# Storing x2's rows: two DMAs of 64 partitions in place of one with an outermost dimension of 2

## The chip, the cores and the metric

The kernel runs on one core of a Trainium2 chip. The metric is the device time of one execution in microseconds, the median of three runs. Before the change it is 1280.42 us (1277.43 to 1281.81).

## The reference

Three stages, one behind the other. Attention over 4 batches of 8 heads, 1152 positions and 64 features, with queries that are means of two neighbours (so 576 of them); a product stage (a * b) @ w3 @ w_out; and eight experts, to which 2304 tokens are assigned greedily by their logits, 288 each.

```python
# attention
q_pool = q.reshape(B, H, S // 2, 2, D).mean(axis=3)
attn = softmax(q_pool @ k.T / sqrt(D))            # written out in the reference
x = (attn @ v).transpose(0, 2, 1, 3).reshape(2304, 512)
# products
x = ((x @ w1) * (x @ w2)) @ w3 @ w_out            # 512 -> 1024 -> 1024 -> 512
# experts: every expert gets cap = 2304 / 8 tokens, in the order of the logits
logits = x @ w_gate
for idx in argsort(-logits.flatten()):
    tok, e = idx // 8, idx % 8
    if assigned[tok] < 0 and counts[e] < cap: assigned[tok] = e; counts[e] += 1
for e in range(8):
    out[assigned == e] = relu(x[assigned == e] @ w1[e]) @ w2[e]
```

## The kernel before

All products are made from operands split into a high and a low part (three matmuls for one product). Every operation is recorded with the buffers that it reads and writes, and a list scheduler (class `Sched`) orders all of them with rough costs and latencies that are written at each `sch.op`; they are then emitted in order of their modelled start. So each engine has a fixed order, and a changed cost or latency moves the order of operations on all engines. Nearly all instructions of this part are recorded through one helper, so the profile puts them on line 113, and they are told apart by the names of their tiles.

The part that the change touches stands between the product stage and the experts. `x2 = h @ W`, with W = w3 @ w_out, is made in 18 tiles of 128 tokens (`x2_part`). A tile's products add up in a bank (`pb`), ACT copies it to a buffer `x2o` of three (`r_xo`), and SP stores it to DRAM twice: the left 256 columns to `x2a`, all 512 columns to `x2` (the profile calls it `x`). The rows of a tile are two groups of 64, whose tokens lie 9 rows apart in DRAM, so a store had the pattern [2, 64, width] on the DRAM side and 128 partitions on the other. The last three tiles (15, 16, 17) are made half by half: first the left columns of each, then the right columns of 16, 17 and 15 (`late`), whose operands for tile 15 are split once more by ACT (`x2h`) and DVE (`x2l`).

The experts fetch their tokens' rows from DRAM with gathers that POOL issues. The first expert's rows come in halves: three gathers from `x2a` into `early`, which need every row of `x2a`, and three from `x2` (by `idx_right`) into `g`, which need every row of `x2`. PE transposes them, ACT and DVE split them (`exh`, `exl`), and the products of seven groups of features with the left half are placed ahead of the transposes of the right half (`AHEAD`). Gathers of the weights (`u`) stand behind them on POOL.

All along, the greedy assignment (`routing`, tiles `rt_...`) runs beside it: seven phases, each with eight rounds in which DVE makes a mask, PE counts (`rt_oh`, `rt_mask`), DVE reduces, PE sums (`rt_own`), and DVE takes the next threshold; then `rt_rows`, and a list of an expert's tokens (`sl_...`) which gives `idx`. Four phases end by the end of x2, the other three beside the experts. Each engine takes its instructions in order, so a routing product waits on PE behind what stands ahead of it, and the other way round.

The lines of the profile for the parts below are those of the kernel printed here.

Of the kernel before, what the change touches and what calls it, by code (L numbers as in the profile page):

```python
# [11 lines left out]
F32 = mybir.dt.float32  # L12
# [5 lines left out]
OP = mybir.AluOpType  # L18
AX = mybir.AxisListType
PSUM = bass.MemoryType.PSUM  # L20

B, H, S, D = 4, 8, 1152, 64
SP = S // 2
# [11 lines left out]
class Region:  # L35
    """a tile pool that opens and closes while the ops are emitted; its tiles are made at their first use"""
# [36 lines left out]
class LazyTag(Lazy):  # L73
    """a tile of a tag, whose buffers are used in turn"""
# [11 lines left out]
class TagRing:  # L86
    """the buffers of a tag, in turn; the ops that touch the tiles first keep the tiles' order"""
# [4 lines left out]
    def next(self, shape, dt, name, key):  # L92
        """a tile whose ops know it by key and (key, 1), and those keys of the tile that had its buffer before"""
        self.keys.append(key)
        n = len(self.keys) - 1
        free = [self.keys[n - self.bufs], (self.keys[n - self.bufs], 1)] if n >= self.bufs else []
        return LazyTag(self.region, shape, dt, name, self.tag, self.bufs), free
# [20 lines left out]
class LazyCore:  # L118
    """the engines of the core, taking Lazy tiles as operands"""
# [21 lines left out]
class Slots:  # L141
    """n buffers given out while the emission is ordered"""
# [5 lines left out]
class Hold:  # L148
    """one use of a buffer of Slots: taken by its first op, given back after its last"""
# [13 lines left out]
class Sched:  # L163
    """Orders the emission: ops are created in program order with the buffers they read and write;
    run() list-schedules them on the engines with rough costs and emits them by start time."""
# [9 lines left out]
    def ctl(self, fn, labels=(), after=()):  # L175
        """runs fn while emitting, once every op with one of the labels has been emitted"""
        gate, self.gate = self.gate, []
        o = self.op("CTL", 0.0, fn, after=after, lat=0.0)
        self.gate = gate
        o.label = "ctl"  # L180
        o.sdeps = {x for x in self.ops if x.label in labels}
        return o
# [162 lines left out]
def attention(nc, tc, sch, pool, prep, s_pt, s_s, ident, xT, rsum, q, k, v):  # L345
    """xT[4*b + hp][:, s*64 + p] = attention rows of heads (2hp, 2hp+1), query p*9+s of batch b."""
# [54 lines left out]
    def both(ps, hi, lo, src, n, r, kh, kl, pr, scale=None):  # L401
        """hi and lo of scale * src in PSUM; each of several places (place, key) gets them from there"""
# [12 lines left out]
    def prepare_q(p, pr):  # L415
        """qst[p][:, x, h]: q's high part over its low part (x = 0), or the other way round, for s = 0..3, 5..8;
        diag[p]: the high and the low part of both heads' s = 4, each head in its quarter"""
# [9 lines left out]
        # pairs of rows are added, transposed (s above s+5), scaled by -1/16 = -(1/2)(1/8), and split  # L427
# [25 lines left out]
        if first:  # L453
            for g in range(2):
# [14 lines left out]
                # the other head's by way of SBUF; the bank's readers take turns only once  # L469
# [27 lines left out]
        # columns: s = 0..3 (above 5..8) of the one head, then of the other  # L497
# [11 lines left out]
    def prepare_k(p, pr):  # L509
        """kst[p, h]: rows of k's high part over its low part; khl[p]: the high and the low part, head 1 below head 0"""  # L510
# [3 lines left out]
        if p == 0:  # L514
            # the first head's by itself, which is there sooner
# [54 lines left out]
    def tile_ops(p, j, sm, pr):  # L570
# [14 lines left out]
        for c in range(3):  # L585
# [5 lines left out]
            sch.label = "prep" if j == 4 else "attn"  # the ops that read the tiles of the preparation  # L591
# [7 lines left out]
            # the copy that finds the row's least value on its way  # L599
# [8 lines left out]
        for g in range(3):  # L608
# [25 lines left out]
            if (j, g) in RAW:  # L634
                # by way of a copy in SBUF, which frees the vector engine
# [136 lines left out]
NCG = 6           # columns of tokens whose counts one matmul takes  # L772
# [3 lines left out]
def routing_consts(nc, pool, spare):  # L776
    """constants of the routing, made on the chip, by way of a buffer that is not in use yet"""
# [13 lines left out]
    nc.vector.tensor_scalar(tri, jp, 0.0, None, op0=OP.is_le)          # [p', p]: p' >= p  # L791
    c["tris"] = tris = pool.tile([128, 128], BF16, name="rc_tris")
    nc.vector.tensor_scalar(tris, jp, 0.0, None, op0=OP.is_gt)         # [p', p]: p' < p
# [18 lines left out]
    # of the counts [(a, t), (a', e)] those with a = a'; and each row's own threshold  # L812
# [14 lines left out]
    # thresholds of the first round: the keys as float bits  # L827
# [4 lines left out]
    # rows (in token order) of column c*128+p: 576*b + 9*(p%64) + s with (b, s) = divmod(2*c + p//64, 9)  # L832
# [20 lines left out]
def routing(nc, sch, rp, slots, c, L, keyL, A, rows_of, idx, prio, prio_l):  # L853
    """Greedy assignment, in which every expert gets N/8 tokens: A[p, e, c] = 1 where token c*128+p goes to expert e.

    Every phase fills an expert. The n-th in the order of filling has its weights in rows rows_of[n][p, k] of 1024
    values, and idx[n][r, g] = row of its token 96*g + r."""
# [32 lines left out]
    def pick(n):  # L890
        """the n-th expert: the first one that is full and not taken yet"""
# [10 lines left out]
    for ph in range(8):  # L902
# [18 lines left out]
        if ph < 7:  # L921
            # the counts lack what the experts can take
            dve(120, lambda: nc.vector.tensor_scalar(
                own8[96:97], rem[96:97, None, :].to_broadcast([1, NTHR, 8]), 4096.0, -1.0, op0=OP.min, op1=OP.mult), [keyR], ["own8r"])
            base = kb = None  # float bits of the lower end of the range that holds the threshold
# [143 lines left out]
def slot_lists(nc, sch, rp, slots, c, A, idx, prio, prio_l):  # L1069
    """lists(n, own): idx[n][r, g] = row of token 96*g + r of the expert that own (one-hot) names"""  # L1070
# [59 lines left out]
KF = 8           # tiles of 128 of the 1024 hidden features  # L1130
KD = DM // 128
CH = 288         # tokens in a chunk of the first products
NCH = N // CH
LC = 384         # tokens in a chunk of the logits
# [4 lines left out]
def moe_and_experts(tc, sch, env, w1, w2, w3, w_out, w_gate, e1, e2, out):  # L1139
# [13 lines left out]
    def split(hi, lo, src, n, pr, r, wh, wl, hi_e=("ACT", "DVE"), lo_e=("DVE", "POOL"), uses=(), hold=None, free=()):  # L1153
        """hi = src rounded to the matrix unit's 12 bits, lo = src - hi (exact)"""
# [9 lines left out]
    def acc_op(engine, dur, fn, r, hold, first, pr, then=()):  # L1164
        """one of the ops that add up in a bank, for which the buffers in `then` are free already"""
        if first:
            return sch.op(engine, dur, fn, r=r, w=then, takes=hold, prio=pr)
        o = sch.op(engine, dur, fn, r=r, w=[hold], prio=pr)
        o.uses.append(hold)
        hold.users += 1  # L1170
        return o

    # ---- weights that come as float64: their float32 values, made from the words of the float64
# [10 lines left out]
    def convert(w, row, col, blocks, width, pr):  # L1184
        """[128, blocks*width] float32: w[row + 128*j + p, col:col + width] for j in range(blocks)"""
# [11 lines left out]
        # sign, exponent less 896 and 23 bits of the mantissa; what float32 can't hold becomes 0  # L1197
# [27 lines left out]
    def split_x(b, pr):  # L1225
        """x = xhi + xlo; xhi goes to the buffer of a part of x that has been split"""
# [11 lines left out]
    # ---- h = (x @ w1) * (x @ w2), kept whole, and its routing logits  # L1238
# [45 lines left out]
    def logits(f, c, pr):  # L1284
        """rows 16*c.. of one bank: the stationary is w_gate's columns between columns of zeros"""
# [13 lines left out]
    # w_gate seen from the hidden features: Wg = w3 @ (w_out @ w_gate)  # L1299
# [10 lines left out]
    def project(nm, weight, copy, rows_n, cols, stat, stat_key, put_hi, put_lo, dst_key, step):  # L1310
        """hi | lo of weight @ (stat hi + lo); the parts of w_out, and those of w3 transposed, go to DRAM as well"""
# [71 lines left out]
    lg_part = lambda c, n: lg.rearrange("p c t -> p (c t)")[:LW, c:c + n].bitcast(F32)  # noqa: E731  # L1383
    sch.op("ACT", c_act(LC), lambda: evac("ACT", lg_part(0, LC), lg_ps.tile[:LW, :LC]), uses=[lg_ps], w=[klg], prio=P_H)

    # ---- routing beside W = w3 @ w_out and x2 = h @ W
# [4 lines left out]
    # the logits leave the region of the products before it closes  # L1391
# [27 lines left out]
    # W  # L1419
# [38 lines left out]
    # x2, its rows in token order in DRAM  # L1458
# [4 lines left out]
    whole = [(x, m) for m in range(KF) for x in ("Wh", "Wl")]  # what all but two tiles wait for, as W needs banks too  # L1463
    r_xh, r_xl = ring(xr, "x2h", 2, [128, KF, 128], F32R), ring(xr, "x2l", 2, [128, KF, 128], F32R)
    r_xo = ring(xr, "x2o", 3, [128, DM], F32)
    LAST = N // 128 - LATE  # the last tiles are made half by half, so that the first expert's rows are there sooner

    def x2_part(t, h, n, xs, xo, pr):
        """columns h * n.. of the rows of tile t"""
# [12 lines left out]
        for dst, w, width, key in ((x2a, DM // 2, DM // 2, "x2a"), (x2, DM, n, "x2")):  # L1482
            def fn(dst=dst, w=w, width=width, at=b * SP + s_, step=(b1 - b) * SP + s1 - s_):
                nc.sync.dma_start(dram(dst, at * w + h * n, [[step * w, 2], [NS * w, 64], [1, width]]), xo[:, h * n:h * n + width])
            if key == "x2" or not h:
                sch.op("DMA", 600, fn, r=[(kxo, h)], w=[(key, t, h)], prio=pr, lat=2500)
# [21 lines left out]
    # ---- the experts  # L1508
# [13 lines left out]
    def unit(w, n, k, pr):  # L1522
        """rows rows_of[n][:, k] of w, split: the tiles of the two halves of the parts, and their keys"""
# [47 lines left out]
    def gather(e, pr):  # L1571
        xh, kxh = r_xh()
        xl, kxl = r_xl()
        # the rows' halves: [h][j] = place, key
# [33 lines left out]
    def expert(e, xs, wu, pr):  # L1608
# [42 lines left out]
        # the last expert's rows go out as soon as the last of their quarters is there  # L1651
# [23 lines left out]
    # the first expert's rows come half by half  # L1675
# [8 lines left out]
    for e in range(8):  # L1684
        if e + 1 < 8:
            xs[e + 1] = gather(e + 1, P_E + e + 0.4)
            wu_next = lambda e=e: expert_w(e + 1, P_E + e)  # noqa: E731
# [14 lines left out]
NX = B * KD       # x in parts of [128 features, one batch]  # L1702
# [7 lines left out]
AHEAD = 7          # groups of features that the first halves of the first expert's rows keep busy  # L1710
HELD = 4           # loads of weights that the gathers of the first expert's rows don't have to wait for
LATE = 3           # tiles of x2 made half by half
# [57 lines left out]
```

## Time and profile before

| what | value |
|---|---|
| time, median of three runs | 1280.42 us (1277.43 to 1281.81) |
| profiled execution, span from first to last instruction | 1286.7 us (no time around it is given) |
| PE busy | 1176.8 us, 91% |
| DVE busy | 1033.4 us, 80% |
| SP's stores of x2 | 837.6 to 975.8 us of the span |
| stretch in which the experts start | from 978.9 us |
| mean granted clock of PE | 0.965 |

The profiled execution is 6.3 us longer than the median of the runs, so positions in the trace are read as positions in it, and a difference is carried over to the median. A row of a timeline gives start and length, and in brackets how long the engine was idle ahead of it and what ended that. SP rows are the issue of a DMA; a long one means that SP was held while issuing. The granted clock is 1.00 at 2.4 GHz and 0.50 at 1.2 GHz.

### The profile page before, as it was taken

How to read it: one execution, taken by the hardware profiler on the slowest of the kernel's cores; microseconds unless marked ns; L12 is line 12 of the kernel's file. 1: busy time of each engine (PE TensorE's matmuls, PEld its weight loads, DVE VectorE, ACT ScalarE, POOL GpSimd, SP SyncE). 2: the span in 40 equal slices, each digit the busy share in tenths (PEclk: the TensorE clock that was granted, in tenths of full speed). 3: DMA queues.
4: the chain of work that ended last, by engine and by line, in shares of the span. 5: the costliest groups of instructions: out<-in, count | busy, mean ns of one | idle time of the engine just before them, and what ended most of it. 6: DMA issues, size and time to landing. Idle time of an engine off the chain costs nothing.

```text
span 1286.7 us, 23991 instructions
## 1 busy us (share of the span) xinstructions
PE 1176.8 (91%) x8377; PEld 1106.5 (86%) x8377; DVE 1033.4 (80%) x2964; ACT 636.6 (49%) x1333; POOL 683.8 (53%) x704
## 2 busy tenths in 40 slices
PE   7999999999999999899999999888984978989895
PEld 5999999999999998899999996666673978879895
DVE  7999999999999989988777866777762797978651
ACT  6888888888888886422222102222220443432330
POOL 4566666666666655444322533454423786763860
PEclk9999999999999999899999999999996999988998
DMA  9676766666766531254655234411113545552440
GB/s 211 150 180 149 156 159 155 155 145 148 155 145 156 117 73 57 83 189 164 196 174 182 72 122 138 127 59 51 51 51 104 162 150 170 179 169 68 138 150 19
DMA packets 115445, 169.85 MB, mean 132 GB/s; under 512 B 46789, under 2 KB 78540, under 8 KB 115324
## 3 DMA queue, kind: packets, MB, share of 16 engines
q1 hardware_dynamic: 102940, 125.32, 37.2%
q0 software_dynamic: 12384, 43.00, 10.6%
q8 instruction: 66, 1.08, 0.4%
q14 instruction: 55, 0.45, 0.1%
HBM read 104.87 MB, written 24.45 MB: 101 GB/s over the span
## 4 chain that ended last, share of the span: by engine, by line
PE 68%; DVE 19%; DMA 4%; issue 3%; SPq 2%; POOL 2%; ACT 1%; POOLq 0%; DVEq 0%; ACTq 0%
PE pb L113 29%; PE s L590 11%; PE pt L614 7%; PE pt L113 6%; PE pt L664 6%; PE s L664 5%; PE s L614 3%; DMA u<-in_moe_w_dram,rows 2%; DVE ul L113 2%; SPq L113 2%; DVE cv_v L113 1%; DVE p L600 1%; DVE rt_own L113 1%; DVE sl_oh L113 1%; DVE rt_flag L113 1%
## 5 line engine op out<-in xcount | busy, mean ns | idle before, releaser
L600 DVE TENSOR_SCALAR_CACHE_REDUCE p<-s 128x384 f32<-128x384 f32 x432 | 229.7, 550 | 34.5 <-PE pt L614 12.0
L590 PE MATMUL s<-kst,qst 128*128 128x384 f32 x768 | 199.3, 358 | 4.8 <-DVE p L600 3.2
L605 ACT ACTIVATE p<-p,mn 128x1152 f32<-128x1152 f32 x144 | 181.2, 1258 | 25.0 <-DVE mn L603 22.8
L113 PE MATMUL pb<-xhi,wh 128*128 128x288 f32 x512 | 156.6, 306 | 1.7 <-ACT wh L113 1.7
L113 PE MATMUL pb<-xlo,wh 128*128 128x288 f32 x512 | 152.3, 297 | 3.3 <-DVE xlo L113 3.3
L113 PE MATMUL pb<-xhi,wl 128*128 128x288 f32 x512 | 152.0, 297 | 1.4 <-DVE wl L113 1.4
L590 PEld LDWEIGHTS s<-kst,qst 128*128 128x128 f32 x768 | 122.9, 190 | 11.1 <-DVE p L600 9.7
L614 PE MATMUL pt<-ident,p 128*128 128x128 f32 x879 | 132.1, 272 | 0.3 <-ACT p L605 0.3
L648 DVE TENSOR_TENSOR p_lo<-pt,p_hi 128x384 fp32r<-128x384 f32 x230 | 124.5, 550 | 0.7 <-ACT p_hi L331 0.7
L331 ACT ACTIVATE p_hi<-pt 128x384 fp32r<-128x384 f32 x230 | 106.7, 493 | 11.3 <-PE pt L614 11.1
L614 PEld LDWEIGHTS pt<-ident,p 128*128 128x128 f32 x879 | 106.8, 140 | 4.4 <-ACT p L605 0.5
L113 DVE SCALAR_TENSOR_TENSOR cv_v<-cv_raw,cv_v 128x512 int32<-128x512 int32 (+1 forms) x120 | 102.1, 856 | 6.9 <-POOL cv_raw L113 4.9
L113 PEld LDWEIGHTS pb<-xlo,wh 128*128 128x128 f32 x512 | 97.3, 190 | 4.1 <-DVE xlo L113 4.1
L113 PEld LDWEIGHTS pb<-xhi,wh 128*128 128x128 f32 x512 | 97.2, 190 | 2.5 <-ACT wh L113 1.9
L113 PEld LDWEIGHTS pb<-xhi,wl 128*128 128x128 f32 x512 | 97.2, 190 | 1.8 <-DVE wl L113 1.8
L341 POOL TENSOR_TENSOR p_lo<-praw,p_hi 128x384 fp32r<-128x384 f32 x96 | 96.9, 1018 | 0.4
L113 ACT ACTIVATE a<-pb 128x288 f32<-128x288 f32 x64 | 26.2, 410 | 133.0 <-PE pb L113 126.8
L335 POOL CAST p_hi<-praw 128x384 fp32r<-128x384 f32 x96 | 47.6, 506 | 81.9 <-ACT praw L331 81.9
L113 POOL TENSOR_TENSOR cv_raw<-cv_raw 128x512 f32<-128x512 f32 x40 | 43.2, 1079 | 86.3 <-DVE cv_v L113 67.1
L113 POOL DMA_INDIRECT u<-in_moe_w_dram,rows x64 | 73.6, 1150 | 27.1 <-issue 8.6
L113 PE MATMUL pb<-ehh,uh 128*128 128x288 f32 x256 | 80.7, 315 | 0.0
L113 ACT ACTIVATE uh<-u 128x1024 fp32r<-128x1024 f32 (+1 forms) x66 | 55.4, 861 | 51.1 <-DMA u<-in_moe_w_dram,rows 50.8
(317 smaller groups left out, 3479.5 us busy)
## 6 DMA issues: line engine op xcount, KB each, us to landing
cv_raw<-in_moe_w_dram SPq DMA_DIRECT2D x32, 512.0 KB
vr<-in_v_dram SPq DMA_DIRECT2D x32, 288.0 KB
kr<-in_k_dram SPq DMA_DIRECT2D x32, 288.0 KB
kst<-kH SPq DMA_DIRECT2D x31, 288.0 KB
kst<-kL SPq DMA_DIRECT2D x31, 288.0 KB
qr<-in_q_dram SPq DMA_DIRECT2D x15, 576.0 KB
w3t<-wg SPq DMA_DIRECT2D x16, 512.0 KB
w<-w3t SPq DMA_DIRECT2D x16, 512.0 KB
```

Source lines behind the costliest of these rows:

```text
L113: return f(*[x.get() if isinstance(x, Lazy) else x for x in a], **{n: x.get() if isinstance(x, Lazy) else x for n, x in k.items()})
L331: nc.scalar.activation(out, in_, AF.Copy)
L335: nc.gpsimd.tensor_copy(out, in_)
L341: (nc.vector if eng == "DVE" else nc.gpsimd).tensor_tensor(out, a, b, op=OP.subtract)
L590: nc.tensor.matmul(ps.tile[:, :384], a[:, :], b[:, cs], start=(n == 0), stop=(n == len(passes) - 1))
L600: sch.op("DVE", c_dve(384), lambda ps=ps, c=c, cs=cs: nc.vector.tensor_scalar(t[:, cs], ps.tile[:, :384], 1.0, BIG, op0=OP.mult, op1=OP.mi ...
L605: sch.op("ACT", c_act(S, psum=False, acc=True), lambda: nc.scalar.activation(t, t, AF.Exp, bias=mn[:, 3:4], scale=-1.0, accum_out=sm[0][:, ...
L614: nc.tensor.transpose(ps.tile[:, a * 128:(a + 1) * 128], t[:, b * 128:(b + 1) * 128], ident)
L648: sch.op("DVE", c_dve(384), lambda view=view, src=src: nc.vector.tensor_tensor(view(lo), src(), view(hi).bitcast(F32), op=OP.subtract), us ...
L664: nc.tensor.matmul(ps.tile[:, :n], vt[:, t, :, :], src[half][:, t, off:off + n], start=(half == 0 and t == 0), stop=(half == 1 and t == NT ...
```

## The change

In `x2_part` the store with a pattern of [2, 64, width] becomes two stores of 64 partitions each, with the rows as outermost dimension. The cost in the scheduler becomes 500 with a latency of 2300, where it was 600 and 2500. Both stores are recorded as writing the same key, so the scheduler takes the second of a pair to depend on the first, and emits it later. Else the diff removes comments and docstrings, which emit nothing.

```diff
         for dst, w, width, key in ((x2a, DM // 2, DM // 2, "x2a"), (x2, DM, n, "x2")):
-            def fn(dst=dst, w=w, width=width, at=b * SP + s_, step=(b1 - b) * SP + s1 - s_):
-                nc.sync.dma_start(dram(dst, at * w + h * n, [[step * w, 2], [NS * w, 64], [1, width]]), xo[:, h * n:h * n + width])
-            if key == "x2" or not h:
-                sch.op("DMA", 600, fn, r=[(kxo, h)], w=[(key, t, h)], prio=pr, lat=2500)
+            if key == "x2a" and h:
+                continue
+
+            for rows, at in ((slice(0, 64), b * SP + s_), (slice(64, 128), b1 * SP + s1)):
+                def fn(dst=dst, w=w, width=width, rows=rows, at=at):
+                    nc.sync.dma_start(dram(dst, at * w + h * n, [[NS * w, 64], [1, width]]), xo[rows, h * n:h * n + width])
+                sch.op("DMA", 500, fn, r=[(kxo, h)], w=[(key, t, h)], prio=pr, lat=2300)
```

The end of SP's stores, tiles 15 to 17 (their buffers are x2o0, x2o1 and x2o2), before:

```order
L113 DMA x2a_217<-x2o0_9760 2x64x256 [waits DMAHW1_49,Activation_49]
L113 DMA x2_216<-x2o0_9760 2x64x256 [waits DMAHW2_49]
L113 DMA x2a_217<-x2o1_9818 2x64x256 [waits DMAHW3_49,Activation_49]
L113 DMA x2_216<-x2o1_9818 2x64x256 [waits DMAHW4_49]
L113 DMA x2a_217<-x2o2_9877 2x64x256 [waits DMAHW5_49,Activation_49]
L113 DMA x2_216<-x2o2_9877 2x64x256 [waits DMAHW6_49]
L113 DMA x2_216<-x2o1_9818 2x64x256 [waits DMAHW7_49,Activation_49]
L113 DMA x2_216<-x2o2_9877 2x64x256 [waits DMAHW0_49,Activation_49]
L113 DMA x2_216<-x2o0_9760 2x64x256 [waits DMAHW1_49,Activation_49]
```

and now, from the first store of tile 17's left columns on:

```order
L113 DMA x2a_217<-x2o2_9881 64x256 [waits DMAHW5_49,Activation_49]
L113 DMA x2a_217<-x2o1_9820 64x256 [waits DMAHW6_49]
L113 DMA x2_216<-x2o1_9820 64x256 [waits DMAHW7_49]
L113 DMA x2_216<-x2o2_9881 64x256 [waits DMAHW0_49]
L113 DMA x2_216<-x2o1_9820 64x256 [waits DMAHW1_49,Activation_49]
L113 DMA x2a_217<-x2o2_9881 64x256 [waits DMAHW2_49]
L113 DMA x2_216<-x2o2_9881 64x256 [waits DMAHW3_49]
L113 DMA x2_216<-x2o2_9881 64x256 [waits DMAHW4_49,Activation_49]
L113 DMA x2_216<-x2o1_9820 64x256 [waits DMAHW5_49]
L113 DMA x2_216<-x2o2_9881 64x256 [waits DMAHW6_49]
L113 DMA x2_216<-x2o0_9760 64x256 [waits DMAHW7_49,Activation_49]
L113 DMA x2_216<-x2o0_9760 64x256 [waits DMAHW0_49]
```

A wait named Activation is for the copy of a new half tile; DMAHW is for the store eight places ahead. Before, the last left-half store waits for its own copy alone. Now its second part (x2a from x2o2, sixth row) stands behind a store of tile 16's right columns, which waits for that copy.

PE where x2 ends and the first expert begins, before:

```order
L113 MATMUL pb_6478<-Wh,x2l_9184 128x256
L113 MATMUL pb_6478<-Wh,x2h_9171 128x256
L113 MATMUL pb_6478<-Wl,x2h_9171 128x256
L113 MATMUL pb_6478<-Wh,x2l_9184 128x256
L113 MATMUL pt_65<-ident,early 128x96 x3
L113 MATMUL pt_67<-ident,early 128x96 x3
L113 LDWEIGHTS rt_mask_9280
L113 MATMUL pt_66<-rt_oh_9232,rt_mask_9280 90x48
```

and now:

```order
L113 MATMUL pb_6478<-Wh,x2l_9184 128x256
L113 LDWEIGHTS rt_mask_9280
L113 MATMUL pt_65<-rt_oh_9232,rt_mask_9280 90x48
L113 LDWEIGHTS rt_mask_9280
L113 MATMUL pt_65<-rt_oh_9232,rt_mask_9280 90x48
L113 LDWEIGHTS rt_mask_9280
L113 MATMUL pt_65<-rt_oh_9232,rt_mask_9280 90x48
L113 MATMUL pt_67<-ident,early 128x96 x3
L113 MATMUL pt_66<-ident,early 128x96 x3
L113 LDWEIGHTS rc_ones_145
L113 MATMUL pt_68<-rt_own_9188,rc_ones_145 128x120
```

A round of routing (`rt_mask`, then `rt_own`) that stood behind the transposes of the first gathered rows stands around them. Up to the transposes PE's order is otherwise the same; behind them, routing stands earlier among the products of the experts: the last three `rt_rows` come after 201, 549 and 864 of the 1,536 products, where it was 258, 618 and 969. ACT, DVE and POOL follow with their parts.

## Rows read from the trace of the kernel before

**Rows 1.** page of the profile, first part and chain of waits

```profile
PE 1176.8 (91%) x8377; PEld 1106.5 (86%) x8377; DVE 1033.4 (80%) x2964; ACT 636.6 (49%) x1333; POOL 683.8 (53%) x704
PE 68%; DVE 19%; DMA 4%; issue 3%; SPq 2%; POOL 2%; ACT 1%; POOLq 0%; DVEq 0%; ACTq 0%
```

**Rows 2.** stretches: length, busy us (count) per engine, granted clock, DMA share, GB/s

```profile
660.00:680.00 20.00, 20.00 (x171) 19.66 (x170) 14.65 (x27) 4.72 (x10) 4.30 (x5) 1.00 0.61 195
860.00:880.00 20.00, 16.48 (x93) 12.69 (x92) 18.23 (x64) 4.61 (x8) 8.87 (x9) 0.99 0.14 51
960.00:970.00 10.00, 5.13 (x29) 4.63 (x29) 6.19 (x30) 2.10 (x6) 0.00 (x0) 0.74 0.14 50
970.00:980.00 10.00, 0.42 (x1) 0.18 (x1) 0.00 (x0) 0.00 (x0) 3.74 (x6) 0.50 0.23 74
```

**Rows 3.** timeline of the SP queue: start us, length us, store issued

```profile
837.59 0.58 SPq L113 DMA_DIRECT2D x2a<-x2o  x1
838.22 0.50 SPq L113 DMA_DIRECT2D x<-x2o  x1
962.60 2.58 SPq L113 DMA_DIRECT2D x2a<-x2o  x1
965.22 10.57 SPq L113 DMA_DIRECT2D x<-x2o  x4
```

**Rows 4.** tile x2o: issue lengths of its stores, ns min/median/max

```profile
L113 SPq DMA_DIRECT2D x<-x2o x21: 494/2572/4871, 838.2 to 973.3; - x21
L113 SPq DMA_DIRECT2D x2a<-x2o x18: 478/486/3291, 837.6 to 962.6; - x18
```

**Rows 5.** timeline of ACT, in brackets idle time ahead and its releaser

```profile
959.75 0.38 ACT L113 ACTIVATE x2o<-pb 128x256 f32<-128x256 f32 x1 [7.52 <-DMA x<-x2o]
966.30 0.38 ACT L113 ACTIVATE x2o<-pb 128x256 f32<-128x256 f32 x1 [4.59 <-PE pb L113]
```

**Rows 6.** timeline of PE, end of x2 and start of the experts

```profile
956.98 0.28 PE L113 MATMUL pb<-Wl,x2h 128*128 128x256 f32 x1
957.10 0.28 PE L113 MATMUL pb<-Wh,x2l 128*128 128x256 f32 x1
960.70 0.38 PE L113 MATMUL pb<-Wh,x2h 128*128 128x256 f32 x1 [3.32 <-ACT x2h L113]
978.85 0.42 PE L113 MATMUL pt<-ident,early 96*128 96x96 f32 x1 [12.58 <-DMA early<-x2a,idx]
981.39 0.90 PE L113 MATMUL pt<-ident,early 96*128 96x96 f32 x4 [0.77 <-DMA early<-x2a,idx]
995.85 0.74 PE L113 MATMUL pt<-ident,g 96*128 96x96 f32 x3 [2.02 <-issue]
```

**Rows 7.** timeline of POOL, the gathers of the first expert

```profile
974.04 0.95 POOL L113 DMA_INDIRECT early<-x2a,idx  x1 [19.21 <-DMA x2a<-x2o]
985.58 0.93 POOL L113 DMA_INDIRECT g<-x,idx_right  x1 [7.09 <-issue]
```

**Rows 8.** timeline of DVE, routing around the same place

```profile
961.29 0.30 DVE L113 TENSOR_TENSOR rt_oh<-rt_t,rt_mx 128x144 bf16<-128x144 f32 x1
966.75 0.43 DVE L113 TENSOR_TENSOR rt_mask<-rt_mu,rt_thr 128x270 bf16<-128x270 f32 x1
982.34 0.89 DVE L113 TENSOR_TENSOR exl<-pt,exh 128x288 fp32r<-128x288 f32 x2 [14.28 <-ACT exh L113]
995.51 0.28 DVE L113 TENSOR_REDUCE rt_any<-pt 128x15 f32<-128x120 f32 x1 [3.52 <-remote]
```

**Rows 9.** waits of the SP queue over the span: us in total, times, longest

```profile
SPq L734 <- DMA rsum<-rT: 21.2, 15, 1.5
```

**Rows 10.** waits of PE from 980 us on: us in total, times, longest

```profile
PE pt L113 <- DVE rt_own L113: 9.1, 6, 3.4
PE pt L113 <- DVE rt_mask L113: 4.3, 2, 2.2
PE pt L113 <- DVE rt_rows L113: 3.2, 1, 3.2
```

## What I expect, and why

> **What bounds the kernel now.** I read the page first: PE is busy 91% of the span and holds 68% of the chain that ended last [rows 1]. That is a mean over stages, so I went on to the stage that the change touches, by stretches, and then to the timelines of SP, ACT, PE, POOL and DVE there.
>
> From about 860 us the DMA engines carry the stores of x2 and next to nothing else, at 0.14 of the 16 engines and 51 GB/s, and at 960 us it is still 0.14 and 50 GB/s [rows 2]. 0.14 x 16 is 2.2 engines. In another stretch the same engines moved 195 GB/s at a share of 0.61 [rows 2], so some 50 GB/s is not what the memory gives; it looks like a store that two engines carry. The SP queue shows the backlog: the first two stores are issued in 0.58 and 0.50 us, the last left-half store takes 2.58 us, and the four stores behind it hold SP for 10.57 us [rows 3]. Over all stores the issue of x2 has a median of 2572 ns and a least value of 494 ns [rows 4]: SP is held back by a full queue and not by the instruction.
>
> Three waits hang on that backlog. ACT waits 7.52 us for an x2o buffer at 959.75 us [rows 5], and since the split of the last half tile is queued behind it, PE stands still for 3.32 us before 960.70 [rows 6]. POOL's first gather waits for x2a until 974.04 us [rows 7], so PE waits 12.58 us for its rows, and in 970 to 980 us PE is busy 0.42 of 10 us at a granted clock of 0.50 (1.2 GHz) [rows 2, 6]. The second gather can only start at 985.58 us [rows 7], some 10 us after SP had issued the last store (975.79). Routing stands still as well: rt_mask is ready at 967.2 us, but its product is queued on PE behind the transposes of the gathered rows, and DVE sits idle for 14.28 us before 982.34 [rows 8].
>
> **The change part by part.** *More issues.* 39 stores become 78 [rows 4], so 39 more issues at 0.48 to 0.5 us, some 19 us of SP time over a stage of 140 us in which SP does nothing else. It costs nothing as long as the three to five issues behind one evacuation (2.5 us) end before the next evacuation, and those come some 3 us apart in the half tiles (24 products, 0.12 us from one to the next [rows 6], is 2.9 us).
>
> *The width of a store.* No row shows a store of 64 rows of x2. From below: the small store rsum is waited for by the next instruction of SP for 21.2 / 15 = 1.4 us [rows 9], so 1.4 us behind its issue is the least. From above: 64 x 256 floats (65 KB) at the old 50 GB/s are 1.3 us of transfer on top of that, 2.7 us, and with the full backlog of before the landing comes 974.04 - 965.18 = 8.9 us behind the issue [rows 3, 7]. I take 2.3 us: the small store, with some transfer.
>
> The Trainium skill speaks for and against this. Its page "DMA: Bandwidth & Descriptors", section "Rules for kernel authors", says that two transfers to disjoint halves of the partitions don't pay, since both run on the same 16 engines, and to use one of 128 partitions; by that rule the sum is nothing. The same page, section "Why a DMA increments its semaphore by 16 and not by 1", says that the number of engines is the largest up to 16 that divides the outermost size of both sides; by that rule the store of before has 2, that of after 16, and the sum stands. The 2.2 engines of the stretches agree with the second for the store of before; no run shows the 64-row store yet.
>
> *The ACT wait goes.* The buffers come free early, ACT evacuates right behind PE, and the split is there in time. PE goes on at 957.2 instead of 960.70 us, and the last 24 products end near 961 us (2.9 us, with the routing products between them some 3.8).
>
> *The last left-half store.* PE's row ends at 957.1 us after two second halves of 24 products each, so the last left half was ready near 951.3 us. In the new order of SP its second store stands behind a store that waits for the evacuation of tile 16's second half: products until 954.2 us, evacuation of 0.38 us [rows 5], so about 955. Issue of that one and of this one: 956.0. Landing 2.3 us later, 958.3; POOL gathers at 958.5 instead of 974.04, 15.5 us earlier. The transposes' last rows came 981.39 - 974.04 = 7.35 us behind the first gather [rows 6, 7], so 965.9 instead of 981.39. The new order has rt_mask's products ahead of them on PE. rt_oh to rt_mask took 961.29 to 967.18, 5.9 us [rows 8]; with the split no longer in its way, rt_oh comes near 957, rt_mask near 963, before the rows. That costs nothing and fills the wait.
>
> *The second gather.* Products end at 961, evacuation 961.4, two issues 962.4, landing 964.7, in place of 985.58: 20.9 us earlier. POOL is through with the first three gathers by then (three issues of 0.95 us [rows 7] from 958.5 us on).
>
> *What lies between.* From the last transposes of the first halves to the first of the second halves, before took 995.85 - 981.39 = 14.5 us [rows 6], with 3.52 us in which DVE was idle before rt_any [rows 8], whose end freed the bank for those transposes. If this stretch keeps its length, 15.5 us is all that is gained. If it shrinks until the second gather is the limit (995.85 - 985.58 = 10.3 us behind it, so 975.0), it is 20.9. The shorter idle time on PE favours the higher clock, the extra routing step in the new order favours the full length. I take the middle, 18 us. Weight loads of the first expert are queued behind these gathers on POOL and come earlier by as much, and everything behind is an in-order continuation on PE.
>
> *Sum.* The profiled span is 1286.7 us and no time around it is given; it lies 6.3 us over the median of the runs. 1286.7 - 18 = 1268.7 for the span, 1280.42 - 18 = 1262.4 for the runs.
>
> **The rivals.** *Given back to routing.* The new order places routing earlier among the 1,536 products of the experts: the three last rt_rows stand behind 201, 549 and 864 of them, before behind 258, 618 and 969. A product of 288 columns takes 0.12 x 288 / 256 = 0.135 us, so PE comes to those steps 7.7, 9.3 and 14.2 us sooner. Before, PE waited 9.1 + 4.3 + 3.2 = 16.6 us for routing there [rows 10]. For it: DVE has to keep up with a shorter distance. Against: DVE gets its 14.28 us back, and the experts reached last get their rows sooner. At half of 14.2 us the gain is 18 - 7 = 11 us, 1269; at all of it 4 us, 1276.
>
> *More than I take.* The second gather is the limit and the stretches at the lower clock are gone: 20.9 us, and up to 6 more if the 10.3 us behind the second gather shrink as well, which at half the clock they can by up to one half; 24 us in the middle, about 1256. For it: the clock of 0.50 [rows 2]; against: the routing steps in between.
>
> *The store gets no wider.* If halves share what one had, the backlog stays, the bytes are the same and 19 us of issue are hidden: 1280. That is what the rule on disjoint halves (the Trainium skill, "DMA: Bandwidth & Descriptors", Rules for kernel authors) would make of it. Against it: 2.2 engines with another stretch at 195 GB/s.
>
> *Slower.* Routing becomes the bound on PE. Three phases with eight rounds of two products are up to 48 places where PE waits in order. If each waits 0.38 us longer, the 18 us are gone; from there it decides, and at 0.6 us each (29 us) the time is 1291. Against it: before, only 10 of such waits are listed at all [rows 10].
>
> **How the numbers follow.** My forecast (1257 to 1268): 0.58. More: 0.12 (1250 to 1257). Given back to routing: 0.20 (1268 to 1276). No wider: 0.05. Slower: 0.05. The range of 1253 to 1273 leaves out the far end of "more", the last part of "given back", and the last two, some 0.2. A difference of 0.3% (3.8 us) is about what a measurement of this kernel can tell from no change. Faster by more than that: 0.90; within it 0.05; slower 0.05.
>
> **What would show it.** In the changed profile: issues of the stores near 0.5 us throughout; a DMA share in short bursts instead of 0.14 without end; no wait of ACT for x2o; the first gather near 958 to 960 us and PE's wait for its rows at 3 to 6 us; the second gather near 965 us; PE's waits for routing not above 25 us in all behind it. I am wrong if the share stays at 0.14, if the first gather comes after 965 us, if the landing of a 64-row store takes above 5 us, or if the rows come as early as I say and the experts' part is longer than before by what was gained.

## The result, and the profile after

The changed kernel takes 1259.8 us (median of four runs, 1255.25 to 1264.11), where the kernel before takes 1279.12 us in the same comparison: a ratio of 0.9843, interval 0.9816 to 0.987. That is 19.3 us less; 18 were predicted (1262.4 us). The profiled spans are 1286.7 and 1262.3 us, 24.4 apart; the span before lies 7.6 us above its median and the one after 2.5 us, so some 5 us of that difference belong to the two profiled executions, and a term that is read from the two traces is uncertain by as much.

The page after (first part and chain, as [rows 1]; under it three stretches, as [rows 2]):

```profile
PE 1175.4 (93%) x8377; PEld 1107.6 (88%) x8377; DVE 1037.6 (82%) x2958; ACT 640.4 (51%) x1333; POOL 692.0 (55%) x710
PE 71%; DVE 20%; DMA 3%; issue 2%; POOL 2%; SPq 1%; ACT 1%; POOLq 0%; DVEq 0%; ACTq 0%
```

```profile
860.00:880.00 20.00, 16.45 (x94) 12.50 (x92) 17.93 (x63) 4.92 (x9) 8.88 (x9) 1.00 0.26 60
960.00:970.00 10.00, 7.85 (x53) 7.08 (x52) 6.74 (x29) 1.14 (x3) 7.54 (x9) 0.66 0.29 82
970.00:980.00 10.00, 8.14 (x52) 7.53 (x51) 7.33 (x21) 2.71 (x4) 6.11 (x6) 0.83 0.65 210
```

The DMA share of the stage has gone up from 0.14 to 0.26 at 860 us, with 60 GB/s in place of 51: the stores are no longer spread out behind each other. They come in bursts, and the share is a mean over bursts and pauses. Two short stretches of the changed kernel show the width itself, the first with nothing but the first store of x2 (its 64 x 256 floats are all that is moved there):

```profile
839.20:839.80 0.60, 0.60 (x5) 0.41 (x3) 0.60 (x1) 0.00 (x0) 0.60 (x1) 1.00 0.46 109
840.00:840.50 0.50, 0.13 (x1) 0.00 (x0) 0.50 (x3) 0.00 (x0) 0.50 (x2) 1.00 0.96 209
```

One 64-row store by itself stands at a share of 0.46, which is 7.4 engines' worth in the mean, and with the next ones behind it the share is 0.96, or 15.4 engines' worth; the old stores stood at 2.2. In stretches this short the count is rough, but it is far above two engines.

At 970 us PE is busy 8.14 of 10 us where it was 0.42, and the 210 GB/s are above all the first expert's weights, which before were asked for from 989 us on.

The stores: the timeline of SP near the end, and the tile x2o with its issues and the time from issue to landing (as [rows 3, 4]):

```profile
954.95 0.59 SPq L113 DMA_DIRECT2D x2a<-x2o  x1
955.59 6.13 SPq L113 DMA_DIRECT2D x<-x2o  x6
```

```profile
L113 SPq DMA_DIRECT2D x<-x2o x42: 445/596/1313, 838.7 to 961.1; - x42
L113 SPq DMA_DIRECT2D x2a<-x2o x36: 445/541/598, 838.1 to 955.0; - x36
DMA to landing us min/median/max: 1.9/2.1/2.6
```

An issue now takes 0.596 us in the median for x2 (2.572 before). The row that answers to the 10.57 us of the four last stores of before is the last one of SP: six stores in 6.13 us, and that with the pauses for the last two copies in it. A store lands 2.1 us behind its issue, and no more than 2.6.

ACT's copies, POOL's gathers and PE's transposes (as [rows 5 to 7]):

```profile
951.05 0.39 ACT L113 ACTIVATE x2o<-pb 128x256 f32<-128x256 f32 x1 [2.85 <-PE pb L113]
960.23 0.38 ACT L113 ACTIVATE x2o<-pb 128x256 f32<-128x256 f32 x1 [2.92 <-PE pb L113]
```

```profile
957.77 0.95 POOL L113 DMA_INDIRECT early<-x2a,idx  x1 [3.42 <-DMA x<-x2o]
964.09 0.94 POOL L113 DMA_INDIRECT g<-x,idx_right  x1 [0.88 <-ACT exh L113]
```

```profile
961.27 0.31 PE L113 MATMUL pt<-rt_oh,rt_mask 128*90 128x48 bf16 x3 [1.08 <-DVE rt_mask L113]
961.90 0.30 PE L113 MATMUL pt<-ident,early 96*128 96x96 f32 x1 [0.21 <-DMA early<-x2a,idx]
963.00 0.90 PE L113 MATMUL pt<-ident,early 96*128 96x96 f32 x4 [0.79 <-DMA early<-x2a,idx]
974.40 0.47 PE L113 MATMUL pt<-ident,g 96*128 96x96 f32 x3 [0.38 <-DVE rt_any L113]
```

For its copies ACT waits for PE and for nothing else (tile 17's left half is copied at 951.05, before at 959.75). The first gather starts at 957.77 us (974.04), the second at 964.09 (985.58), the transposes of the right halves at 974.40 (995.85). PE's wait of 12.58 us for the first rows is down to 0.21 and 0.79 us: what PE does at 961.27, ahead of the rows, is a step of routing.

DVE there, and what PE waited for behind it (as [rows 8, 10]; the second list is from 960 us on, that of before from 980):

```profile
956.50 0.30 DVE L113 TENSOR_TENSOR rt_oh<-rt_t,rt_mx 128x144 bf16<-128x144 f32 x1
960.73 0.48 DVE L113 TENSOR_TENSOR rt_mask<-rt_mu,rt_thr 128x270 bf16<-128x270 f32 x1
974.07 0.28 DVE L113 TENSOR_REDUCE rt_any<-pt 128x15 f32<-128x120 f32 x1 [0.30 <-PE pt L113]
```

```profile
PE pt L113 <- DVE rt_mask L113: 7.7, 4, 3.1
PE pt L113 <- DVE rt_own L113: 5.1, 6, 1.5
PE pt L113 <- DVE rt_oh L113: 3.8, 1, 3.8
PE pt L113 <- DVE rt_al L113: 2.7, 1, 2.7
PE pt L113 <- DVE rt_rows L113: 1.2, 1, 1.2
```

The mask that lay ready for 15 us before is used at once, and of DVE's idle 14.28 us the longest stretch left here is 2.24 us.

The last row of the result starts 24.5 us earlier (1251.1, before 1275.6; the first line is that of before):

```profile
L113 POOL DMA_INDIRECT out_dram<-eo,idx x24: 907/924/1750, 1028.6 to 1275.6; - x24
L113 POOL DMA_INDIRECT out_dram<-eo,idx x24: 908/938/1370, 1007.6 to 1251.1; - x24
```

21.45 of the 24.5 us are there when the second transposes start; the experts behind them took 276.7 us (1251.1 - 974.4) after 279.7.

### The profile page after: what moved, and what is told of

Its sections match the earlier page's. It is cut to its first block, busy times and chain, and to the rows that moved or that the text cites. A ratio compares the mean times of both kernels' runs of the same rounds, so it can differ in the third digit from the quotient of the medians.

```text
span 1262.3 us, 24072 instructions
## 1 busy us (share of the span) xinstructions
PE 1175.4 (93%) x8377; PEld 1107.6 (88%) x8377; DVE 1037.6 (82%) x2958; ACT 640.4 (51%) x1333; POOL 692.0 (55%) x710
## 4 chain that ended last, share of the span: by engine, by line
PE 71%; DVE 20%; DMA 3%; issue 2%; POOL 2%; SPq 1%; ACT 1%; POOLq 0%; DVEq 0%; ACTq 0%
PE pb L113 30%; PE s L590 12%; PE pt L614 7%; PE pt L113 6%; PE pt L664 6%; PE s L664 5%; PE s L614 3%; DVE cv_v L113 2%; DVE rt_own L113 2%; DVE rt_flag L113 1%; DVE sl_oh L113 1%; DVE rt_base L113 1%; DMA u<-in_moe_w_dram,rows 1%; DVE rt_mask L113 1%; DVE p L600 1%
## 5 line engine op out<-in xcount | busy, mean ns | idle before, releaser
L605 ACT ACTIVATE p<-p,mn 128x1152 f32<-128x1152 f32 x144 | 181.1, 1257 | 23.3 <-DVE mn L603 21.3
L113 POOL TENSOR_TENSOR ul<-u,uh 128x512 fp32r<-128x512 f32 (+1 forms) x42 | 75.7, 1807 | 25.6 <-ACT uh L113 18.7
L113 POOL DMA_INDIRECT u<-in_moe_w_dram,rows x64 | 69.8, 1090 | 23.8 <-issue 10.3
```

The lines of the kernel that those rows point to most:

```text
L113: return f(*[x.get() if isinstance(x, Lazy) else x for x in a], **{n: x.get() if isinstance(x, Lazy) else x for n, x in k.items()})
L605: sch.op("ACT", c_act(S, psum=False, acc=True), lambda: nc.scalar.activation(t, t, AF.Exp, bias=mn[:, 3:4], scale=-1.0, accum_out=sm[0][:, ...
```

## The experiments

Eight kernels ran in two groups, the first four on one chip and the last four (from the 62 rows on) on another. The kernel before ran beside them, with medians of 1290.01 and 1290.62 us: that is 0.9% above the 1279.12 us of the first comparison, so the times are read by their ratio to it. The expectations call the eight e1 to e8, in the order in which they stand here.

The theory was that the old store ran on two engines and left a backlog, and that only the width of the store matters. The rivals were the order of instructions, which the changed costs move on all engines, and two transfers in flight in place of one.

### Width without the order

One recorded operation with the old cost issues both stores, so PE, DVE, ACT and POOL have the order of before.

```diff
-            for rows, at in (...):
-                def fn(...): nc.sync.dma_start(...)
-                sch.op("DMA", 500, fn, ..., lat=2300)
+            def fn(dst=dst, w=w, width=width):
+                for rows, at in (...):
+                    nc.sync.dma_start(...)
+            sch.op("DMA", 600, fn, ..., lat=2500)
```

> Both 64-partition stores of a pair are issued from one recorded operation with the old cost (600, latency 2500), so that PE, DVE, ACT and POOL keep the order of the kernel before; only the stores are the changed ones. Theory (width: a store of 64 rows runs on many engines, the backlog goes): first gather at 956 to 960 us, PE's wait for its rows under 6 us, second gather near 964 us, time 1257 to 1264 us. Rival (order: the gain comes from routing placed earlier among the experts' products): 1274 to 1281 us with PE's order of before.

Measured: ratio 0.9828 (0.9795 to 0.9861), 1267.79 us (by the ratio 1257 us on the scale of the expectation). The interval overlaps that of the changed kernel (0.9816 to 0.987): the order gives nothing that can be measured here, where a few us could hide, and the width gives the gain without it. The gathers (POOL) and the first transposes of each half (PE):

```profile
950.32 0.96 POOL L113 DMA_INDIRECT early<-x2a,idx  x1 [0.32 <-issue]
960.31 1.49 POOL L113 DMA_INDIRECT g<-x,idx_right  x1 [2.10 <-DMA x<-x2o]
```

```profile
956.41 0.66 PE L113 MATMUL pt<-ident,early 96*128 96x96 f32 x6
972.44 0.74 PE L113 MATMUL pt<-ident,g 96*128 96x96 f32 x3 [4.17 <-DVE rt_any L113]
```

Here the last left-half store stands in front of the right halves, and the first gather starts at 950.32 us, some 4 us sooner against the last copy of x2o than in the changed kernel (956.6 and 960.2 us in the two traces), and before the 956 to 960 us that I had said. No gain of it shows in the time: PE takes the rows as it comes to them, and waits 4.17 us for a step of routing before the second transposes.

### The order without the width

The changed kernel's order and 78 issues, each half a store by columns, with the outermost dimension of 2 as before.

```diff
-                    nc.sync.dma_start(dram(dst, at * w + h * n, [[NS * w, 64], [1, width]]), xo[rows, h * n:h * n + width])
+                    nc.sync.dma_start(dram(dst, at * w + h * n + c * wd, [[step * w, 2], [NS * w, 64], [1, wd]]),
+                                      xo[:, h * n + c * wd:h * n + c * wd + wd])
```

> The order of the changed kernel with its 78 issues, but each store is halved by columns instead of by rows: both halves keep the outermost dimension of 2. Theory (width): DMA share 0.13 to 0.15 from 860 us on, the first gather not before 970 us, time 1274 to 1284 us. Rival (order, or two transfers in flight instead of one): 1257 to 1266 us, first gather before 962 us.

Measured: ratio 1.0092 (1.0063 to 1.0122), 1302.0 us, slower than before. In absolute time that is 18 us past the upper end that I gave; by the ratio it is 1291 us on the scale of the expectation, 7 us past it. Two stretches and the gathers:

```profile
900.00:920.00 20.00, 17.87 (x80) 13.25 (x79) 17.02 (x64) 4.74 (x9) 8.27 (x10) 0.91 0.14 47
940.00:960.00 20.00, 17.12 (x128) 15.99 (x126) 11.50 (x45) 2.92 (x6) 4.28 (x4) 0.91 0.14 47
```

```profile
987.20 0.96 POOL L113 DMA_INDIRECT early<-x2a,idx  x1 [30.34 <-DMA x<-x2o]
996.97 0.94 POOL L113 DMA_INDIRECT g<-x,idx_right  x1 [5.31 <-DMA x<-x2o]
```

The share is 0.14 again, now at 47 GB/s with the shorter rows, so the backlog is longer: the first gather starts at 987.20 us. Both rivals fall: neither the order nor twice as many transfers gives the gain.

### An outermost dimension of 4

```diff
-                    nc.sync.dma_start(dram(dst, at * w + h * n, [[NS * w, 64], [1, width]]), ...)
+                    nc.sync.dma_start(dram(dst, at * w + h * n, [[16 * NS * w, 4], [NS * w, 16], [1, width]]), ...)
```

> The changed kernel in every order, but the 64 rows of a store are written as 4 x 16, so its outermost dimension is 4. If the outermost dimension sets the number of engines, the stores run on 4: 100 GB/s while one runs, and landing 1.4 us plus 0.7 us (64 KB) to 1.3 us (128 KB) behind the issue if nothing is ahead, 2.5 to 4 us where pairs queue. A tile's 393 KB come every 6 to 7 us, some 60 GB/s, so no backlog builds up but at the half tiles at the end: time 1259 to 1266 us, landing median clearly above the 2.1 us of the changed kernel. If any split into 64 rows frees the store whatever the outermost size: landing 2.1 us and 1260 us.

Measured: ratio 0.9849 (0.9801 to 0.9897), and the landing of the changed kernel:

```profile
DMA to landing us min/median/max: 1.9/2.1/2.4
```

This tells nothing of 4 engines. The 4 x 16 rows have one stride, and in the built program the store has 64 rows again: all five engines' orders are the same as those of the changed kernel, word for word. So it is a second measurement of the changed kernel, beside 0.9843, and a scale for the traces: from the second transposes to the last row of the result this one took 283.4 us, that of the first profile, on another chip, 276.7. A true outermost 4 was not measured.

### Twice as many issues

As the first, with four stores of 32 rows.

```diff
-                for rows, at in (...64 rows each...):
+                for r0, at in ((0, ...), (32, ... + 32 * NS), (64, ...), (96, ... + 32 * NS)):
+                    nc.sync.dma_start(dram(dst, at * w + h * n, [[NS * w, 32], [1, width]]), xo[r0:r0 + 32, ...])
```

> As e1 (orders of the kernel before on PE, DVE and ACT), with four stores of 32 partitions instead of two of 64: 156 issues. If issues are hidden (the prediction's step), 36 issues behind the first half tile at 0.5 to 0.6 us end near 963 us, the second gather comes near 965 us, and the time is that of e1 within 3 us. If SP's issues are what comes next, every tile's eight issues (4 to 5 us) push the last store out by 5 us or more and the time is 4 us or more above e1.

Measured: ratio 0.9857 (0.9809 to 0.9906), which the first kernel's interval overlaps. Its issues, and the gathers:

```profile
L113 SPq DMA_DIRECT2D x<-x2o x84: 302/419/1107, 839.5 to 960.9; - x84
```

```profile
954.39 1.06 POOL L113 DMA_INDIRECT early<-x2a,idx  x1 [2.25 <-DMA x2a<-x2o]
963.28 1.09 POOL L113 DMA_INDIRECT g<-x,idx_right  x1 [2.49 <-DMA x<-x2o]
```

156 issues cost nothing that can be measured, the second gather starts at 963.28 us, and an issue of 32 rows is even shorter (0.419 us).

### Rows outermost, but 62 of them

This one holds the theory against its nearest rival, that any store with its rows outermost is spread out.

```diff
-                for r0, at in (...):
+                for r0, m, at in ((0, 62, ...), (62, 2, ...), (64, 62, ...), (126, 2, ...)):
+                    nc.sync.dma_start(dram(dst, at * w + h * n, [[NS * w, m], [1, width]]), xo[r0:r0 + m, ...])
```

> As e1 (orders of the kernel before on PE, DVE, ACT), rows outermost, but each group of 64 rows is stored as 62 and 2 rows, so 156 issues. If the number of engines is the largest up to 16 that divides the outermost size (2 for 62 and for 2), the backlog of the kernel before is back in spite of rows outermost: DMA share 0.13 to 0.15 from 860 us on, first gather after 968 us, second after 978 us, time within 1% of the kernel before. If any store with its rows outermost spreads over the engines: time of e4 (156 issues, 0.986 of before), first gather before 958 us.

Measured: ratio 1.0031 (1.0012 to 1.005). Two stretches, the issues, the gathers:

```profile
860.00:880.00 20.00, 16.24 (x93) 12.21 (x92) 18.16 (x66) 3.89 (x7) 9.17 (x9) 1.00 0.13 50
900.00:920.00 20.00, 16.92 (x92) 12.80 (x91) 17.26 (x61) 4.52 (x8) 8.07 (x9) 0.91 0.14 51
```

```profile
L113 SPq DMA_DIRECT2D x<-x2o x84: 224/266/982, 836.4 to 977.8; - x84
```

```profile
972.76 0.96 POOL L113 DMA_INDIRECT early<-x2a,idx  x1 [21.15 <-DMA x<-x2o]
984.47 0.94 POOL L113 DMA_INDIRECT g<-x,idx_right  x1 [7.25 <-DMA x<-x2o]
```

The share is 0.13 to 0.14 at 50 and 51 GB/s, as before the change, with the gathers at 972.76 and 984.47 us. The rule of the Trainium skill ("DMA: Bandwidth & Descriptors", Why a DMA increments its semaphore by 16 and not by 1) says that the largest number up to 16 that divides the outermost size of both sides decides the number of engines, which makes 2 for 62 rows and 16 for 64; this run agrees at 2.1 to 2.2 engines, and the changed kernel's share of 0.96 fits the 16. So the gain does not come from rows as such. Sizes whose divisor lies between 2 and 16 were not run. The rule of the same page of the Trainium skill against halves of the partitions (Rules for kernel authors) did not hold here: the store that it would keep had an outermost size of 2.

### Which of the stores

As the first, with the old store for tiles 12 to 17, and then with the old store for tiles 0 to 11.

```diff
             def fn(dst=dst, w=w, width=width):
+                if t >= 12:        # in the second kernel: t < 12
+                    nc.sync.dma_start(dram(dst, ..., [[((b1 - b) * SP + s1 - s_) * w, 2], [NS * w, 64], [1, width]]), xo[:, ...])
+                    return
```

> As e1, but the last six tiles keep the old store (outermost dimension 2), and only tiles 0 to 11 have the pair. Queue theory: the queue is empty when tile 12 is stored (927 us), then 50 GB/s: 393 KB of a tile take 7.9 us, half of that for a half tile's two stores (5.2 us), so the last left half lands near 966 us and the last store near 977 us. First gather 964 to 968 us, second 974 to 979 us, about half of the gain lost: ratio 0.990 to 0.994. Rival (what the backlog of the whole stage does, not the end): nearly all of the gain, first gather before 960 us.

> As e1, but only the last six tiles have the pair, and tiles 0 to 11 keep the old store. Queue theory: 12 x 393 KB at 50 GB/s are done by 932 to 936 us, before the half tiles begin, so all of the gain is there: first gather 950 to 959 us, second 960 to 965 us, ratio 0.980 to 0.986 as e1. Rival (backlog of the first twelve counts): ratio above 0.990.

Measured: 0.9917 (0.9885 to 0.9949) with the old store at the end, 0.9862 (0.9824 to 0.99) with it at the beginning. The gathers of the first:

```profile
968.86 0.95 POOL L113 DMA_INDIRECT early<-x2a,idx  x1 [14.37 <-DMA x<-x2o]
980.37 0.93 POOL L113 DMA_INDIRECT g<-x,idx_right  x1 [7.07 <-issue]
```

and two stretches and the gathers of the second:

```profile
900.00:920.00 20.00, 17.68 (x79) 13.06 (x78) 16.33 (x61) 4.81 (x9) 8.27 (x10) 0.91 0.14 51
940.00:960.00 20.00, 18.36 (x157) 17.69 (x156) 16.64 (x72) 4.71 (x11) 7.90 (x8) 1.00 0.37 89
```

```profile
953.72 0.96 POOL L113 DMA_INDIRECT early<-x2a,idx  x1 [0.40 <-DMA x<-x2o]
963.48 1.16 POOL L113 DMA_INDIRECT g<-x,idx_right  x1 [2.43 <-DMA x<-x2o]
```

The queue theory has both: with an empty queue at tile 12, the old store puts the gathers at 968.86 and 980.37 us (0.9 and 1.4 us later than I said), and about half the gain is lost. With the old store in the first twelve tiles, the share is 0.14 in 900 to 920 us, the backlog is gone before the half tiles come, and the gathers start where they do with all stores wide, as seen from the last copy of x2o (959.45 us here, 956.62 in the first kernel). It is the last six tiles' stores that cost; the backlog of the first twelve by itself costs nothing that can be measured (0.9862 against 0.9828, with intervals that overlap). One thing doesn't fit: the trace of the first of the two ends as late as that with 62 rows (1291.8 and 1292.6 us of span), though its runs are 12 us faster in the median (1282.17 and 1294.46), and they scatter from 1276 to 1296 us. The profiled execution, at 1293.57 us, was the second longest of the eight, and its experts took 288.5 us from the second transposes on (992.12 to 1280.6), more than in any other trace read here; why is not known. I take the ratio for its size, and the trace for the places alone.

### What binds now

```diff
-AHEAD = 7
+AHEAD = 6
```

> e1 with AHEAD = 6 in place of 7: one group of the first expert's left-half products fewer stands ahead of the right half's transposes and one bank of the transposes is not held. In e1 PE waits 4.2 us for rt_any before these transposes though the rows are there. If the bank is what binds after the change, this wait goes and the transposes come 2 to 4 us earlier against the last x2o copy (15.8 us in e1), time 0 to 4 us under e1. If the routing step itself binds (the transposes stand behind rt_own in PE's order), the wait stays and the time is that of e1 within noise.

Measured: ratio 0.984 (0.9804 to 0.9876), the first kernel's time. The second transposes on PE, in two threes as before, and PE's waits from 955 us on:

```profile
968.01 0.34 PE L113 MATMUL pt<-ident,g 96*128 96x96 f32 x2
970.91 0.51 PE L113 MATMUL pt<-ident,g 96*128 96x96 f32 x3 [1.97 <-issue]
```

```profile
PE pt L113 <- DVE rt_own L113: 10.0, 7, 3.7
PE pt L113 <- DVE rt_mask L113: 9.0, 7, 2.2
PE pt L113 <- DVE rt_oh L113: 4.3, 2, 3.7
```

The same waits from 955 us on in the first kernel, which has none for `rt_oh`:

```profile
PE pt L113 <- DVE rt_mask L113: 9.4, 6, 3.8
PE pt L113 <- DVE rt_own L113: 8.3, 7, 3.0
```

The seventh group was what held the transposes: without it they start at 968.01 us, 8.7 us behind the last copy of x2o (959.34), where it was 15.8; 2 to 4 us had been expected. Whether its bank or its products held them, this run does not tell apart. Nothing of the 7 us shows in the time. PE no longer waits 4.17 us for `rt_any`, but 10.0 + 9.0 + 4.3 = 23.3 us for the three steps listed, after 9.4 + 8.3 = 17.7, so the waits for routing have moved and not gone. The experts took 282.8 us from there (278.2 in the first kernel). That routing takes the 7 us back is the likely reading and not shown: it rests on one trace of each kernel, from two chips, and 4.6 us is less than the 6.7 us between two traces of one program above.

## Why the prediction was right

- *Two engines and a backlog.* Right: share and rate of before, the long issues, and the same picture whenever the outermost size has no larger divisor than 2 (columns, 62 rows).
- *The ACT wait goes.* Right: the last copy of x2o ends at 960.6 us, 961.4 predicted.
- *The landing of a 64-row store.* Taken as 2.3 us between 1.4 and 8.9; measured 2.1.
- *More issues cost nothing.* Right: issues of 0.541 and 0.596 us, and twice as many again cost nothing either.
- *The last left-half store behind a copy.* Issue predicted to end at 956.0, first gather at 958.5; 955.5 and 957.77 measured. The price of that order, some 4 us for this gather, is real and hidden: with the old order the gather came sooner and the time was the same within the noise.
- *The first transposes.* The term was too small: I kept the 7.35 us from the first gather to the last transposes, and took 15.5 us of gain; the rows came faster (963.00 - 957.77 = 5.2 us), and the gain there was 18.4 us. PE's wait for them, put at 3 to 6 us, was 0.21 + 0.79.
- *The second gather.* 964.7 predicted, 964.09 measured, but by the profile the wait that ended last was not the store: POOL waited 0.88 us until ACT's first split.
- *What lies between.* I took the middle of 15.5 and 20.9. Measured in the traces: 21.45, just past the upper end. Both the length (11.4 us after 14.5) and the start of the stretch had moved. In the runs the whole gain is 19.3 us, 1.3 from the forecast. That it is so near is in part luck: the middle was a choice, the term ahead of it was 2.9 us too small, and the traces overstate the gain of the runs by some 5 us.
- *Given back to routing* was the rival with the most weight, and it did not come at this size: PE waited 7.7 + 5.1 + 3.8 + 2.7 + 1.2 = 20.5 us for the steps listed, after 16.6 for those of before, or 20.9 after 19.1 with `rt_any`, which both lists leave out, although routing stands 57 to 105 products earlier. The first experiment shows nothing of the new order in either direction. At the next step, with the rows 7 us sooner still, it probably did come.
- *More than I take* starts at 20.9 us, which the traces' 21.45 just pass and the runs' 19.3 do not. Its condition did not hold: the lower clock was not gone, with a granted clock of 0.66 from 960 to 970 us, where PE was busy 7.85 us, and 0.83 in the 10 us behind, where it was busy 8.14.
- *No wider* fell with the changed kernel's share and landing, *slower* with its time.
- *Two slips.* The rows cited for *slower* list 9 waits, not 10, and half of the 10.3 us in *more* is 5.2, not 6. Neither enters the forecast.

## What to carry to other kernels

Before anything else on a DMA, look at its outermost dimension, and at the share of the DMA engines while it runs alone: here 0.13 to 0.14 of 16 engines, with a rate that did not move, was a store on two of them. A backlog costs where somebody waits for its end, so the price is read at the last stores and not from the stage's mean. And a wait that goes uncovers the next one: here some 19 us could be had, and the 7 us by which the next step brought the transposes forward did not show in the time.

## What I had not expected

- The time to issue a store is not a matter of its rows alone. It was 0.541 and 0.596 us in the median for 64 rows, 0.420 and 0.419 for 32, and 0.301 and 0.266 for the mix of 62 and 2, but the old store of 128 partitions was issued in 0.478 us where nothing held it, less than one of 64.
- A GB/s costs more of the engines' time with the wide store: 0.26 for 60 GB/s, where it was 0.14 for 51. A share is therefore no measure of bytes.
- Two strides that can be folded into one are folded when the program is built, so a pattern that is written with an outermost 4 can run with 64.
- The same program can differ by 6.7 us between two traces in one stage (283.4 and 276.7 us for the experts, on two chips), so a difference of a few us there has no weight from one trace.
